# The tail h - tanh(h) of a feed-forward layer: a product of two shifted squares from ScalarE in place of a Horner chain on VectorE, and no GpSimd

## The chip, the cores and the metric

The kernel runs on one core of one Trainium2 chip. The metric is the device time of one execution in microseconds (us). Before the change three runs took 1145.72, 1147.4 and 1150.55 us; the median is 1147.4 us. One execution was recorded by the hardware profiler, and all rows below come from it. The engines are named as the profile does: PE is TensorE's matmul, PEld its weight load, DVE VectorE, ACT ScalarE, POOL GpSimd, SP the engine that issues the DMAs.

## The reference, cut to what matters

```
state = zeros(B, H, D, D)                           # B, H, S, D = 4, 8, 768, 48
for t in range(S):                                  # linear attention with a decay per feature
    y[t]  = r[t] @ (state + (u * k[t]) outer v[t])
    state = w[t][:, None] * state + k[t] outer v[t]
x = y, as (B*S, H*D) = (3072, 384)
h = x @ w_in                                        # w_in: 384 x 2048
g = h - tanh(h)
out = g @ w_out                                     # w_out: 2048 x 384
```

Everything is computed in float32. The difference h - tanh(h) loses its digits where h is small, so the kernel uses a series there.

## The kernel before, in words

There are four batches of 768 tokens. For each batch the attention runs over four pairs of heads. A pair computes its scores inside chunks of 128 tokens in levels m = 1, 2, 4, ... 64: at each level PE makes the score blocks (`gram`, L184), DVE takes them into the score matrix under a mask (`take`, L198; for m of 32 and 64 ACT does it with plain copies, L205), then DVE multiplies the decays into r (L219) and POOL into k (L221), and only after that the next level's `gram` can start. Then come transposes of k (L242), their copies by ACT (L243), the chunk states (L248 on PE, L255 and L257 on DVE) and the outputs `yp` (L266, L269), which ACT copies to `y_sb` (L272).

The feed-forward layer works on blocks of 384 tokens, two to a batch. `first` (L285) runs over 16 slices f of 128 hidden features: three float32 matmuls `hp` (L290; each is two passes in the trace, so six rows to a slice), the copy h by ACT (L293), and then the tail that the change touches (L295 to L309), which ends in a tile `gT`. `second` (L313) runs over three groups of 128 tokens: 16 matmuls `op` over all `gT` (L317), the copy `o` by ACT (L320), and the DMA out. PSUM for `hp` and `op` is one pool of two buffers (`ps_d`). The tiles of the tail (h, th, sq, big, o) have three buffers each, `gT` has 18.

The layer of batch b - 1 is laid between the attention of batch b: the first pair stands beside the first block's `first`, the second beside its `second`, and so on. So the execution has four stretches: batch 0's attention with the loading of the weights (about 0 to 206 us), then three batches of attention with the layer of the batch before (206 to 963 us), then the layer of the last batch alone (963 to 1144.7 us). Within a stretch the tile framework's scheduler decides at build time in which order each engine takes its instructions. Each engine then works through its list in that order and waits on semaphores, so an instruction that waits holds up all that stand behind it on its engine.

In this text an "hp stretch" is a stretch of the middle part in which `hp` is computed (beside an even pair), and an "op stretch" one in which `op` is computed (beside an odd pair). There are six of each.

## Time and profile before

| | us | what it is |
|---|---|---|
| median of three runs | 1147.4 | the metric |
| span of the profiled execution | 1144.7 | first to last instruction |
| PE busy | 953.4 (83%) | matmuls, pipelined |
| DVE busy | 849.5 (74%) | |
| POOL busy | 458.1 (40%) | 300.9 of it in L298, the subtraction h - tanh(h) |
| ACT busy | 302.6 (26%) | |
| DMA, mean of its engines | about 11% | q1 moved 40.90 MB |

A share of the whole span is a mean over stretches that differ. The stretch tables below give each engine's busy time in one stretch; the difference to the length of the stretch is that engine's idle time. In a row of instructions the bracket at its end says how long the engine was idle before it and what ended that.

### The profile page before, as it was taken

What the parts mean: (1) busy time and instruction counts of PE and PEld (TensorE: products, weight loads), DVE (VectorE), ACT (ScalarE), POOL (GpSimd) and SP (SyncE); (2) the same over time, 40 slices, a digit from 0 to 9 for tenths busy, and PEclk for the clock granted to TensorE, in tenths of its full rate; (3) what the DMA queues carried; (4) which work ended last, traced back from release to release, by engine and by line L of the source; (5) the groups of instructions that cost most, each with busy time, mean ns of one, the idle gap of its engine ahead of it and who ended that gap; (6) DMA issues with size and microseconds to landing.
All of it is one profiled execution on the core that took longest, in us unless ns stands there. A gap on an engine that the chain in (4) does not pass through costs nothing. (4 is left out here: it accounts for less than half of the span.)

```text
span 1144.7 us, 14496 instructions
## 1 busy us (share of the span) xinstructions
PE 953.4 (83%) x5464; PEld 648.1 (57%) x5464; DVE 849.5 (74%) x1688; ACT 302.6 (26%) x653; POOL 458.1 (40%) x292
## 2 busy tenths in 40 slices
PE   3867667898898879897999799888998789779778
PEld 3767667664565546664666457664666456335334
DVE  6776877899739992799659972899568962990991
ACT  1202112343023411343123401342123303330430
POOL 3332323347314531357223631357224811760670
PEclk9999999999899899998998879998999999899899
DMA  6222232200010002000010001000100000000000
GB/s 234 72 95 88 80 105 88 70 28 1 28 49 15 15 21 76 23 28 1 28 49 29 1 21 36 21 28 0 39 25 1 1 9 13 1 0 21 0 0 21
DMA packets 17749, 41.82 MB, mean 37 GB/s; under 512 B 1808, under 2 KB 7952, under 8 KB 17680
## 3 DMA queue, kind: packets, MB, share of 16 engines
q1 hardware_dynamic: 17680, 40.90, 10.8%
q8 instruction: 43, 0.70, 0.3%
q14 instruction: 26, 0.21, 0.1%
HBM read 36.18 MB, written 4.72 MB: 36 GB/s over the span
## 5 line engine op out<-in xcount | busy, mean ns | idle before, releaser
L298 POOL TENSOR_TENSOR th<-h,th 128x384 f32<-128x384 f32 x128 | 300.9, 2368 | 235.2 <-ACT th L295 235.1
L290 PE MATMUL hp<-xT,w_in_sb 128*128 128x384 f32 x768 | 306.7, 542 | 48.8 <-ACT h L293 48.8
L317 PE MATMUL op<-w_out_sb,gT 128*128 128x384 f32 x768 | 288.9, 525 | 32.9 <-DVE gT L309 16.5
L184 PE MATMUL g<-rp,kq 48*128 48x64 f32 x2304 | 185.0, 317 | 84.3 <-DVE rp L219 48.6
L184 PEld LDWEIGHTS g<-rp,kq 48*128 48x128 f32 x2304 | 171.7, 228 | 132.6 <-issue 69.3
L290 PEld LDWEIGHTS hp<-xT,w_in_sb 128*128 128x128 f32 x768 | 148.5, 206 | 154.8 <-ACT h L293 70.2
L304 DVE SCALAR_TENSOR_TENSOR gT<-gT,sq 128x384 f32<-128x384 f32 x384 | 230.3, 610 | 0.6
L317 PEld LDWEIGHTS op<-w_out_sb,gT 128*128 128x128 f32 x768 | 147.9, 202 | 138.9 <-DVE gT L309 27.3
L221 POOL TENSOR_TENSOR kq<-kq,tot 128x384 f32<-128x384 f32 x96 | 98.0, 1021 | 206.8 <-PE g L184 196.3
L293 ACT COPY h<-hp 128x384 f32<-128x384 f32 x128 | 61.3, 479 | 254.2 <-DVE gT L307 136.2
L198 DVE COPY_PREDICATED scores<-mask,g 128x384 f32<-128x384 uint8 x128 | 79.1, 677 | 66.5 <-PE g L184 64.7
L309 DVE COPY_PREDICATED gT<-big,th 128x384 f32<-128x384 int32 x128 | 97.2, 759 | 18.9 <-POOL th L298 18.6
L300 DVE TENSOR_SCALAR big<-sq 128x384 int32<-128x384 f32 x128 | 68.9, 539 | 39.8 <-ACT sq L297 39.8
L304 DVE SCALAR_TENSOR_TENSOR gT<-sq 128x384 f32<-128x384 f32 x128 | 86.3, 674 | 0.0
L320 ACT COPY o<-op 128x384 f32<-128x384 f32 x24 | 11.5, 479 | 267.9 <-PE op L317 267.9
L219 DVE TENSOR_TENSOR rp<-rp,tot 128x384 f32<-128x384 f32 x96 | 56.1, 584 | 30.9 <-PE g L184 30.7
L221 POOL TENSOR_TENSOR kq<-kq,wt 128x384 f32<-128x384 f32 x16 | 19.5, 1217 | 148.3 <-ACT h L293 62.4
L198 DVE COPY_PREDICATED scores<-mask_even,g 128x384 f32<-128x384 uint8 x32 | 31.0, 1024 | 54.5 <-PE g L184 54.1
L307 DVE SCALAR_TENSOR_TENSOR gT<-gT,h 128x384 f32<-128x384 f32 x128 | 71.0, 555 | 0.2
L295 ACT ACTIVATE th<-h 128x384 f32<-128x384 f32 x128 | 65.9, 515 | 16.3 <-DVE gT L309 15.4
L297 ACT ACTIVATE sq<-h 128x384 f32<-128x384 f32 x128 | 66.5, 519 | 2.6
L269 PE MATMUL yp<-v_sb,scores 128*128 128x48 f32 x384 | 64.6, 298 | 0.0
(54 smaller groups left out, 755.2 us busy)
## 6 DMA issues: line engine op xcount, KB each, us to landing
kq<-in_kT SPq DMA_DIRECT2D x16, 384.0 KB, 3.1
rp<-in_rT SPq DMA_DIRECT2D x16, 384.0 KB, 3.0
wt<-in_wT SPq DMA_DIRECT2D x16, 384.0 KB, 3.1
raw<-in_w_in SPq DMA_DIRECT2D x12, 512.0 KB, 3.9
raw<-in_w_out SPq DMA_DIRECT2D x16, 384.0 KB, 3.1
v_sb<-in_v SPq DMA_DIRECT2D x4, 1152.0 KB, 6.8
out_y<-o SPq DMA_DIRECT2D x24, 192.0 KB, 1.9
u_sb<-in_uT SPq DMA_DIRECT2D x1, 2.0 KB, 1.6
```

The lines of the kernel that those rows point to most:

```text
L184: nc.tensor.matmul(g[h][:, c, :].rearrange("s (b m) -> s b m", m=m), lhsT=lhs[rows, c * L:(c + 1) * L], rhs=rhs, start=True, stop=True)
L198: nc.vector.copy_predicated(out=dst, mask=mask, data=src)
L221: nc.gpsimd.tensor_tensor(out=kv, in0=kv, op=ALU.mult, in1=right.unsqueeze(2).to_broadcast([P, nblk, m]))
L290: nc.tensor.matmul(hp, lhsT=w_in_sb[:, kc, f * P:(f + 1) * P], rhs=xT[:, kc, :], start=(kc == 0), stop=(kc == KC - 1))
L295: nc.scalar.activation(out=th, in_=h, func=AF.Tanh)
L297: nc.scalar.activation(out=sq, in_=h, func=AF.Square)
L298: nc.gpsimd.tensor_tensor(out=th, in0=h, in1=th, op=ALU.subtract)
L300: nc.vector.tensor_single_scalar(big, sq, SMALL, op=ALU.is_gt)
L304: nc.vector.scalar_tensor_tensor(out=g, in0=prev, scalar=c / SERIES[-1], in1=sq, op0=ALU.add, op1=ALU.mult)
L307: nc.vector.scalar_tensor_tensor(out=g, in0=g, scalar=SERIES[-1], in1=h, op0=ALU.mult, op1=ALU.mult)
L309: nc.vector.copy_predicated(out=g, mask=big, data=th)
L317: nc.tensor.matmul(op, lhsT=gs[f][:, i * P:(i + 1) * P], rhs=w_out_sb[:, f, :], start=(f == 0), stop=(f == NF - 1))
```

## The change

Only the tail of `first`, and with it some buffers, is changed. For |h| under 0.5 the old code evaluates a polynomial of degree 4 in s = h * h by Horner's rule: four instructions of the form (x + c) * s and one that multiplies by c4 and h, all on DVE, after a comparison s > 0.25 on DVE which makes the mask; ACT computes tanh and the square; POOL computes h - tanh(h); and DVE puts that difference where the mask is set.

The new code factors the polynomial into two quadratics, each written as a square with a shift plus a constant. ACT computes qa = (s + a1)^2 and qb = (s + a2)^2 with a bias that is read from a small tile, and the mask as Relu(s - 0.25), whose bits are nonzero where s is over 0.25. DVE does three multiplications (c4 * h * s, then times qa + b1, then times qb + b2), the difference h - tanh(h), and the masked copy. POOL has nothing left in the layer. Line numbers grow by 4 to 6 in the new file.

```diff
 SMALL = 0.25
-SERIES = (0.33333332796974213, -0.13333225818814606, 0.05393347775205225,
-          -0.02147073784982366, 0.0069430510383758255)
+SERIES = 0.0069430510383758255
+QUAD = ((0.6848211999739032, 6.0837500747262405), (-2.2310245716004378, 2.349190352486121))
...
+    shift = const.tile([P, 3], F32, name="shift", tag="shift")
+    for i, value in enumerate((QUAD[0][0], QUAD[1][0], -SMALL)):
+        nc.vector.memset(shift[:, i:i + 1], value)
...
-            h = dense.tile([P, NB], F32, name="h", tag="h")
+            def new(name):
+                return dense.tile([P, NB], F32, name=name, tag=name)
+
+            h, th, s, qa, qb, big = (new(n) for n in ("h", "th", "s", "qa", "qb", "big"))
             nc.scalar.copy(out=h, in_=hp)
-            th = dense.tile([P, NB], F32, name="th", tag="th")
+            nc.scalar.activation(out=s, in_=h, func=AF.Square)
+            nc.scalar.activation(out=qa, in_=s, func=AF.Square, bias=shift[:, 0:1])
+            nc.scalar.activation(out=qb, in_=s, func=AF.Square, bias=shift[:, 1:2])
             nc.scalar.activation(out=th, in_=h, func=AF.Tanh)
-            sq = dense.tile([P, NB], F32, name="sq", tag="sq")
-            nc.scalar.activation(out=sq, in_=h, func=AF.Square)
-            nc.gpsimd.tensor_tensor(out=th, in0=h, in1=th, op=ALU.subtract)
-            big = dense.tile([P, NB], I32, name="big", tag="big")
-            nc.vector.tensor_single_scalar(big, sq, SMALL, op=ALU.is_gt)
+            nc.scalar.activation(out=big, in_=s, func=AF.Relu, bias=shift[:, 2:3])
+            hs = new("hs")
             g = gpool.tile([P, NB], F32, name="gT", tag="gT")
-            prev = sq
-            for c in SERIES[-2::-1]:
-                nc.vector.scalar_tensor_tensor(out=g, in0=prev, scalar=c / SERIES[-1], in1=sq,
-                                               op0=ALU.add, op1=ALU.mult)
-                prev = g
-            nc.vector.scalar_tensor_tensor(out=g, in0=g, scalar=SERIES[-1], in1=h,
+            nc.vector.scalar_tensor_tensor(out=hs, in0=h, scalar=SERIES, in1=s,
                                            op0=ALU.mult, op1=ALU.mult)
-            nc.vector.copy_predicated(out=g, mask=big, data=th)
+            nc.vector.scalar_tensor_tensor(out=hs, in0=qa, scalar=QUAD[0][1], in1=hs,
+                                           op0=ALU.add, op1=ALU.mult)
+            nc.vector.scalar_tensor_tensor(out=g, in0=qb, scalar=QUAD[1][1], in1=hs,
+                                           op0=ALU.add, op1=ALU.mult)
+            nc.vector.tensor_tensor(out=th, in0=h, in1=th, op=ALU.subtract)
+            nc.vector.copy_predicated(out=g, mask=big.bitcast(I32), data=th)
...
-            o = dense.tile([P, DM], F32, name="o", tag="o")
+            o = dense.tile([P, DM], F32, name="o", tag="hs")
```

The scheduler puts the new instructions into the lists as follows. First ACT's list near the end of the first block of the last batch's layer, before the change: three instructions to a slice.

```order
L293 COPY h<-hp 128x384
L297 ACTIVATE sq<-h 128x384
L295 ACTIVATE th<-h 128x384
L293 COPY h<-hp 128x384
L297 ACTIVATE sq<-h 128x384
L295 ACTIVATE th<-h 128x384
L320 COPY o<-op 128x384 x3
```

The same place after the change: the copies h of two slices stand together, and the five instructions of each slice follow behind both.

```order
L300 COPY h<-hp 128x384 x2
L301 ACTIVATE s<-h 128x384
L304 ACTIVATE th<-h 128x384
L302 ACTIVATE qa<-s,shift 128x384
L303 ACTIVATE qb<-s,shift 128x384
L305 ACTIVATE big<-s,shift 128x384
L301 ACTIVATE s<-h 128x384
L304 ACTIVATE th<-h 128x384
L302 ACTIVATE qa<-s,shift 128x384
L303 ACTIVATE qb<-s,shift 128x384
L305 ACTIVATE big<-s,shift 128x384
```

So the copies of slices 14 and 15 stand behind the full work of slices 0 to 13, and the work of the last two slices stands behind them. In all of the last batch's first block ACT has 96 instructions where it had 48.

Second PE's list where the first block's `hp` goes over into its `op`, with the attention's matmuls of the second pair of batch 1 between (uk, kmix and kq are the three forms of k that `gram` takes), before the change:

```order
L184 MATMUL g<-rp,uk 128x64 x9
L184 MATMUL g<-rp,kmix 128x64 x12
L290 MATMUL hp<-xT,w_in_sb 128x384 x15
L317 MATMUL op<-w_out_sb,gT 128x384 x23
L184 MATMUL g<-rp,kq 128x64 x12
L317 MATMUL op<-w_out_sb,gT 128x384 x3
```

The same place after the change:

```order
L188 MATMUL g<-rp,uk 128x64 x9
L188 MATMUL g<-rp,kmix 128x64 x4
L294 MATMUL hp<-xT,w_in_sb 128x384 x6
L188 MATMUL g<-rp,kmix 128x64 x8
L323 MATMUL op<-w_out_sb,gT 128x384 x11
L188 MATMUL g<-rp,kq 128x64 x12
L323 MATMUL op<-w_out_sb,gT 128x384 x3
```

The long run of `hp` at the end is cut, and the next pair's first level on kq stands behind 11 matmuls of `op` and no longer behind 23. In the last batch's layer PE's list is as it was: 48 `hp`, 48 `op`, 48 `hp`, 48 `op`, with a few transposes ahead.

## Rows read from the trace of the kernel before

**Rows 1.** Stretch table: PE, PEld, DVE, ACT, POOL busy us; clock; last row six hp stretches.
```profile
334.40:402.50 68.10, 57.83 (x386) 38.30 (x385) 63.85 (x119) 27.28 (x58) 32.77 (x20) 0.95 0.06 21
...
sum 420.10, PE 353.38 PEld 233.79 DVE 383.93 ACT 164.90 POOL 216.62; mean PE 58.90 PEld 38.97 DVE 63.99 ACT 27.48 POOL 36.10
```

**Rows 2.** The same table, two of the six op stretches and the sum of six.
```profile
656.00:718.00 62.00, 59.74 (x319) 39.30 (x319) 30.69 (x69) 9.92 (x24) 16.03 (x9) 0.86 0.09 29
788.00:841.00 53.00, 50.65 (x297) 33.02 (x297) 31.01 (x68) 7.17 (x18) 16.04 (x9) 0.95 0.09 31
...
sum 336.90, PE 315.50 PEld 205.31 DVE 187.16 ACT 47.89 POOL 92.12; mean PE 52.58 PEld 34.22 DVE 31.19 ACT 7.98 POOL 15.35
```

**Rows 3.** Waits over the span: who waited for whom, us in total, times, longest.
```profile
ACT h L293 <- DVE gT L307: 136.2, 65, 5.2
...
ACT y_sb L272 <- PE yp L269: 97.5, 32, 8.6
...
ACT scores L205 <- PE g L184: 55.6, 27, 6.1
...
PE hp L290 <- ACT h L293: 48.8, 30, 3.9
...
PE op L317 <- DVE gT L309: 16.5, 14, 1.8
```

**Rows 4.** Chain that ended last, last batch's layer: start, us, engine, tile, line.
```profile
967.97 0.49 ACT h L293
...
1029.80 25.23 PE op L317 x68
1055.03 3.47 PE hp L290 x11
...
1121.79 19.63 PE op L317 x60
1141.44 0.48 ACT o L320
```

**Rows 5.** Groups by line: busy us, mean ns of one, idle us before.
```profile
L298 POOL TENSOR_TENSOR th<-h,th 128x384 f32<-128x384 f32 x128 | 300.9, 2368 | 235.2 <-ACT th L295 235.1
...
L304 DVE SCALAR_TENSOR_TENSOR gT<-gT,sq 128x384 f32<-128x384 f32 x384 | 230.3, 610 | 0.6
...
L300 DVE TENSOR_SCALAR big<-sq 128x384 int32<-128x384 f32 x128 | 68.9, 539 | 39.8 <-ACT sq L297 39.8
...
L295 ACT ACTIVATE th<-h 128x384 f32<-128x384 f32 x128 | 65.9, 515 | 16.3 <-DVE gT L309 15.4
...
L293 ACT COPY h<-hp 128x384 f32<-128x384 f32 x128 | 61.3, 479 | 254.2 <-DVE gT L307 136.2 <-PE hp L290 74.7 <-POOL th L298 38.6
...
L219 DVE TENSOR_TENSOR rp<-rp,tot 128x384 f32<-128x384 f32 x96 | 56.1, 584 | 30.9 <-PE g L184 30.7
...
L173 ACT ACTIVATE kmix<-kq,u_sb 128x384 f32<-128x384 f32 x16 | 10.4, 650 | 9.3 <-PE g L184 9.3
```

**Rows 6.** Timeline of the last batch's first block: start us, duration us, instruction.
```profile
997.51 0.48 ACT L293 COPY h<-hp 128x384 f32<-128x384 f32 x1 [0.70 <-DVE gT L307]
998.03 0.52 ACT L297 ACTIVATE sq<-h 128x384 f32<-128x384 f32 x1
998.46 0.51 ACT L295 ACTIVATE th<-h 128x384 f32<-128x384 f32 x1
...
1000.88 0.55 DVE L307 SCALAR_TENSOR_TENSOR gT<-gT,h 128x384 f32<-128x384 f32 x1
1001.34 0.55 DVE L304 SCALAR_TENSOR_TENSOR gT<-gT,sq 128x384 f32<-128x384 f32 x1
...
1004.92 1.37 DVE L309 COPY_PREDICATED gT<-big,th 128x384 f32<-128x384 int32 x1 [0.89 <-POOL th L298]
1006.19 1.34 DVE L304 SCALAR_TENSOR_TENSOR gT<-gT,sq 128x384 f32<-128x384 f32 x1
```

**Rows 7.** Timeline, start of the hp stretch that begins at 334.40 us.
```profile
339.54 0.48 ACT L293 COPY h<-hp 128x384 f32<-128x384 f32 x1 [1.50 <-PE hp L290]
```

## The prediction

> **What bounds the kernel now.** I read the stretch tables first. In the middle part (206 to 963 us) PE is on average the busiest engine in the op stretches, and DVE in the hp stretches. An hp stretch takes 70.0 us on average (420.1 / 6) and PE is busy for 58.9 of them, so it stands for 11.1; DVE is busy for 64.0 [rows 1]. An op stretch takes 56.2 us (336.9 / 6), PE is busy for 52.6, DVE for 31.2 [rows 2]. So the hp stretches are the place where PE waits for something, and DVE is what is nearly full there.
>
> The waits say what it is. Over the span PE stood 48.8 us in front of `hp` for the copy h of ACT, and that copy stood 136.2 us for L307, the last arithmetic of the tail on DVE [rows 3]. That chain is a loop through buffers: `hp` needs a PSUM buffer, which the copy h frees; the copy needs one of three tiles h, which DVE frees when it is through with a slice. So PE goes at the pace of DVE's tail once its lead of about five slices is used up. A second sign is the 16.5 us that `op` stood for the last `gT` [rows 3].
>
> The chain of waits shows the same loop undisturbed, in the last batch's layer, where no attention stands beside it. The first copy h starts at 967.97, and the last `gT` of that block releases `op` at 1029.80: 61.8 us for 16 slices, 3.86 us to a slice [rows 4]. ACT's three instructions take about 1.5 us of these, so ACT is idle for more than half [rows 5, 6].
>
> **DVE and POOL.** The tail has seven DVE instructions to a slice, and on the timeline one follows the other after 0.46 us when nothing disturbs (1000.88 to 1001.34), but after 1.27 us where POOL's subtraction runs beside it (1004.92 to 1006.19) [rows 6]. Seven steps of 0.46, with a short one for the comparison, are about 3.1 us; the rest up to 3.86 is what the two engines cost each other. POOL's own subtraction shows a mean of 2368 ns [rows 5].
>
> After the change DVE has five: three of the same form, a TENSOR_TENSOR, and the masked copy. A TENSOR_TENSOR of this shape on DVE has a mean of 584 ns where the other form has 610 [rows 5], so I give it the same step. That is 5 x 0.46 = 2.3 us to a slice, with no POOL subtraction beside it: 1.5 us less than the pace of 3.86. The multiplications of k stay on POOL, so beside attention some of DVE's steps stay long.
>
> **ACT.** It gets six instructions to a slice in place of three. Without an operand from a tile the steps are 0.52 us (h to the square, which waits for it) and 0.43 (square to tanh) [rows 6]. Three of the six read a bias from a tile, which no row of this size shows exactly. From below such a step costs 0.43 like the tanh; from above the nearest row is L173, an ACTIVATE of 128x384 with a scale from a tile and with strides, 650 ns against 515 for the tanh, so 0.135 more [rows 5], and if the steps did not overlap at all, 0.65. I take 0.1 more than the tanh, since part of L173's surplus may be its strides: 0.53 a step. The slice then costs 0.52 + 2 x 0.43 + 3 x 0.53 = 2.97, and as the copies stand in pairs one wait is saved now and then: 2.95 us. The bounds are 2.67 (no surcharge) and 0.52 + 2 x 0.43 + 3 x 0.65 = 3.33; with every instruction at its full mean and no overlap, 0.48 + 2 x 0.52 + 3 x 0.65 = 3.47. So the loop's pace falls from 3.86 to 2.95 us, and its bound moves from DVE (then 2.3) to ACT.
>
> The Trainium skill, "ScalarE: Activation LUTs", section "Rules for kernel authors", says to put relu, add and multiply on VectorE, not on ScalarE; by that rule the mask and the two squares go the wrong way. The trace's row for the comparison on DVE, 539 ns, is no dearer than an ACT instruction, which bears the rule out for the mask [rows 5]. The same page, section "What ACT_TABLE_LOAD costs", gives an ACTIVATE with a pointer bias 280 ns + 0.833 ns per element and an overlap of 93 ns; as an estimate from that page the step is 0.507 us and the slice 2.9, so the sum would be about 1 us less per block. That rule speaks for a better split of the same work; it does not turn the sign, since it is ACT that had time to spare.
>
> **The last batch's layer.** Its first block: the copy of slice 14, after which `op` gets its PSUM buffer, comes after 14 slices of ACT work, 967.97 + 14 x 2.95 + 0.5 = 1009.8. `op` is 96 passes, in the trace's undisturbed row 60 of them take 19.63 us, 0.327 each [rows 4], so 31.4 us and an end at 1041.2, in place of 1055.03. The last `gT` is due at 967.97 + 16 x 2.95 + 1.2 = 1016.4, and `op` reaches it 15 x 0.65 = 9.8 us after its start, at 1019.6, so it does not wait. Gain 13.8. Second block: from the start of `hp` to the end of `op` the old time is 1141.44 - 1055.03 = 86.4 [rows 4]; the new one is 2.5 (six passes and a handoff) + 41.3 + 0.5 + 31.4 = 75.7. Gain 10.7. Together 24 us. `op` is PE alone and nothing of it is saved: that is why 0.9 us a slice over 32 slices, 29 us, does not all come out.
>
> **The middle.** In an hp stretch ACT has, up to the copy of slice 14, 14 x 2.95 = 41.3 us of the tail, and an attention pair's copies, which the op stretches bound at about 7.1 us, as one row of them shows 7.17 us of ACT work in all [rows 2]. The first copy comes 5.1 us after the start (339.54 against 334.40) [rows 7]. ACT takes its list in order, so it also stands where an attention copy waits for PE: now 97.5 us for the outputs and 55.6 for the scores over 16 pairs [rows 3], 9.6 to a pair; being busier it will arrive later, and I take 6. Sum 5.1 + 41.3 + 7.1 + 6 = 59.5, to which I add 1 for handoffs in a list that is now tight: 60.5 in place of 70.0. PE's own 58.9 is the floor just below, so little more is to be had. Six times 9.5 is 57.
>
> In the op stretches PE is bound, and stays so. ACT's last slices spill over into it, and the next pair's first level now stands behind 11 `op` and not 23, which lets the scores start earlier but puts DVE's decay of r behind the tail of slice 14; PE has 7 to 11 matmuls to bridge that, 5 to 7 us, about what the last slices need. The 16.5 us for the last `gT` shrink. I count 3 for all six.
>
> **What costs nothing.** The three memsets of `shift` stand at the start on DVE, long before the first copy h. The tile `o` now shares the ring of hs, so a slice's hs waits for an old output's DMA; the ring was last used a whole block before. Stretch 0 to 206 us has no instruction of the tail. Relu needs no further table: the built list of ACT has one table load, as before.
>
> **Sum.** 57 + 3 + 24 = 84 us. The profiled execution spans 1144.7, the median of the runs is 1147.4, 2.7 more, so 1147.4 - 84 = 1063 us.
>
> **The rivals.** *ACT's list holds the attention back.* ACT now is nearly full in the hp stretches, its copies for the scores, k and y stand behind tail instructions of slices that are not urgent, and PE waits for these copies in front of L248 and L266 rather than for h. For it: the order is fixed at build time with other durations than the chip's. Against: the waits now named L205 and L272 are ACT waiting for PE, not the reverse [rows 3]. If half of the gain in the hp stretches is lost so, and all in the op stretches: 28 + 24 = 52, 1095 us. Chance 0.24.
>
> *PE is never short and keeps its full clock.* Op stretches took 53 us at a mean granted clock of 0.95 and 62 at 0.86 [rows 2]; full is 2.4 GHz and the lower level 1.2 GHz. What sets the clock off these rows don't show; if it is PE's stands before and if they go, the op stretches all take 53: 336.9 - 318 = 19 us. With hp stretches at 57 (the 58.9 with some of it run at the low clock) 78 us, and 26 at the end: 123, 1024 us. Chance 0.13.
>
> *ACT becomes a worse bound than DVE was.* The place is the same loop. Per hp stretch the sum 5.1 + 14 x + 13.1 reaches 70.0 at x = 3.7 us a slice, and in the last batch `op` would start no sooner than the old 1055.03 - 31.4 at x = 3.96; about 3.75 decides, 0.62 us to an ACT instruction. The dearest sum from rows is 3.47, which gives 66.8 and so a gain of 3.2 x 6 + 10 = about 29, 1118 us. For a loss the bias would have to cost more than any row shows: at x = 4.2 each hp stretch takes 7 us more and each last block about 3.5, 42 + 7 = 49 us slower, 1196. Chance 0.05. *No effect*, because PE's stands return in other places: 1147, chance 0.03.
>
> **How the numbers follow.** My forecast has 0.55, the rivals 0.24, 0.13, 0.05 and 0.03. Predicted is 1063 us. The range 1030 to 1102 holds the forecast with both bounds of the bias at nearly their full width and the first rival, and leaves out most of the second and the two that are not faster, about 0.2. A difference under 0.5% (6 us) can't be told from none here. Faster 0.92, same 0.03, slower 0.05.
>
> **What would show it.** ACT's three instructions with a bias at about 0.6 us and steps of 0.53; in the last batch copies h of two slices every 5.9 us and the first `op` near 42 us after the first copy; DVE's steps of the tail at 0.46 throughout there; PE's wait for the copy h, where it is left, ended by ACT's own list and no longer by L307; hp stretches near 60 us and op stretches unchanged. It is wrong if an hp stretch keeps over 65 us, if a slice costs ACT over 3.4, or if PE's waits are named after L205, L243 or L272.

## The result, and the profile after

The changed kernel takes 1042.7 us (median of 4 runs, 1037.1 to 1048.1), the kernel before beside it 1146.6: a ratio of 0.911, 95% interval 0.902 to 0.920. Predicted were 1063 us. The runs of the changed kernel lie at two levels, about 1037 at a mean granted clock of 0.972 and about 1048 at 0.961; the profiled one is of the upper level (1048.07, span 1046.4).

The busy line of the page, kernel after (share of the span, number of instructions):

```profile
PE 924.0 (88%) x5464; PEld 648.8 (62%) x5464; DVE 676.7 (65%) x1435; ACT 479.7 (46%) x1037; POOL 174.5 (17%) x164
```

The span shrank by 98.3 us, of which 29.4 are PE's busy time (953.4 before) with the same 5464 instructions, and 69 are waits. The mean granted clock of the profiled execution was 0.948 before and is 0.961 now, so more of the same passes ran at the full clock.

The stretch table of the kernel after (PE, PEld, DVE, ACT, POOL busy, granted clock), sum of the six hp stretches:

```profile
sum 356.80, PE 334.70 PEld 229.33 DVE 301.24 ACT 276.51 POOL 61.46; mean PE 55.78 PEld 38.22 DVE 50.21 ACT 46.08 POOL 10.24
```

The same view, kernel after, its op stretches: the first of the six, the second, and the sum:

```profile
265.30:332.50 67.20, 64.34 (x340) 43.39 (x338) 24.66 (x57) 12.30 (x27) 7.07 (x7) 0.77 0.09 27
389.10:441.90 52.80, 50.33 (x291) 33.44 (x290) 22.38 (x51) 11.54 (x27) 8.00 (x7) 0.94 0.16 53
...
sum 333.90, PE 318.73 PEld 213.81 DVE 134.88 ACT 71.81 POOL 45.67; mean PE 53.12 PEld 35.63 DVE 22.48 ACT 11.97 POOL 7.61
```

The hp stretches went from 420.1 to 356.8 us [rows 1], the op stretches from 336.9 to 333.9 [rows 2], the last batch's layer (895.6 to 1046.4 us, before 962.8 to 1144.7) from 181.9 to 150.8. ACT's busy time in the hp stretches went up from 165 to 277 us and DVE's went down from 384 to 301. The first op stretch stands out: 67.2 us at a mean clock of 0.77. From 280 to 310 us the granted clock was 0.50, although PE was busy in all of these 30 us. Where a stretch ends can be set a few us earlier or later; with the end of the last `op` as the border in both kernels, the hp stretches lose 64.8 us and the op stretches 2.4.

Waits over the span, kernel after (who for whom: us in total, times, longest):

```profile
ACT h L300 <- PE hp L294: 45.3, 45, 2.2
...
PE g L188 <- DVE rp L223: 31.5, 22, 3.0
...
PE g L188 <- POOL kq L225: 18.9, 10, 2.3
...
PE hp L294 <- ACT h L300: 13.9, 12, 1.3
```

The loop that the prediction found is gone. The 136.2 us in which the copy h stood for DVE's tail [rows 3] have no row any more; the copy now waits for PE, and PE stands 13.9 us for the copy h in place of 48.8. What is left in front of PE is the attention's. Of the 31.5 us for rp, 25.1 lie before 205 us, where nothing was changed. PE's waits in the middle alone, kernel after (205 to 895.6 us), are led by kq from POOL:

```profile
PE g L188 <- POOL kq L225: 13.5, 6, 2.3
PE g L188 <- issue: 9.4, 6, 2.1
PE g L188 <- DVE rp L223: 6.4, 8, 1.9
```

The row "issue" is the stand at the start of the op stretches, shown below. No row there names the copy h: all 13.9 us for it lie in the last batch's layer. Beside attention PE never stands for ACT's tail.

The groups by line, kernel after (busy us, mean ns of one, idle us before it):

```profile
L302 ACT ACTIVATE qa<-s,shift 128x384 f32<-128x384 f32 x128 | 78.3, 612 | 0.0
...
L310 DVE SCALAR_TENSOR_TENSOR hs<-qa,hs 128x384 f32<-128x384 f32 x128 | 70.3, 550 | 2.2 <-ACT qa L302 2.2
...
L304 ACT ACTIVATE th<-h 128x384 f32<-128x384 f32 x128 | 66.3, 518 | 0.0
...
L300 ACT COPY h<-hp 128x384 f32<-128x384 f32 x128 | 57.4, 476 | 45.4 <-PE hp L294 45.3
```

An ACT instruction with a bias from a tile takes 612 ns against 518 without; DVE's form that took 610 ns [rows 5] takes 550 now that no POOL subtraction runs beside it.

Timeline of ACT in the last layer, kernel after (start, duration, instruction; rows of other engines are left out):

```profile
911.85 0.83 ACT L300 COPY h<-hp 128x384 f32<-128x384 f32 x2
...
912.57 0.53 ACT L301 ACTIVATE s<-h 128x384 f32<-128x384 f32 x1
...
913.00 0.52 ACT L304 ACTIVATE th<-h 128x384 f32<-128x384 f32 x1
...
913.41 0.61 ACT L302 ACTIVATE qa<-s,shift 128x384 f32<-128x384 f32 x1
...
913.92 0.61 ACT L303 ACTIVATE qb<-s,shift 128x384 f32<-128x384 f32 x1
...
914.42 0.61 ACT L305 ACTIVATE big<-s,shift 128x384 f32<-128x384 f32 x1
...
914.93 0.52 ACT L301 ACTIVATE s<-h 128x384 f32<-128x384 f32 x1
...
917.27 0.84 ACT L300 COPY h<-hp 128x384 f32<-128x384 f32 x2
```

ACT is never idle here. Two copies h take 0.72 us together (911.85 to 912.57), s to th is 0.43, th to qa 0.41, and each step behind an instruction with a bias 0.50 to 0.51. A pair of slices takes 917.27 - 911.85 = 5.42 us, 2.71 to a slice.

Timeline of PE in the last layer, kernel after:

```profile
917.79 4.14 PE L294 MATMUL hp<-xT,w_in_sb 128*128 128x384 f32 x12 [1.29 <-ACT h L300]
...
939.54 31.23 PE L323 MATMUL op<-w_out_sb,gT 128*128 128x384 f32 x96 [1.30 <-ACT h L300]
...
1011.57 31.23 PE L323 MATMUL op<-w_out_sb,gT 128*128 128x384 f32 x96 [1.30 <-ACT h L300]
```

PE takes two slices in 4.14 us and then stands 1.30 for ACT, ten times in all: 5.44, ACT's pace.

Then the start of an op stretch in the middle, kernel after, DVE and PE rows of the timeline:

```profile
730.58 4.68 PE L323 MATMUL op<-w_out_sb,gT 128*128 128x384 f32 x14
...
736.20 0.56 DVE L312 SCALAR_TENSOR_TENSOR gT<-qb,hs 128x384 f32<-128x384 f32 x1
...
736.67 0.56 DVE L223 TENSOR_TENSOR rp<-rp,wt 128x384 f32<-128x384 f32 x1
...
737.33 2.83 PE L188 MATMUL g<-rp,kq 48*128 48x64 f32 x24 [2.08 <-issue]
...
740.09 5.50 PE L323 MATMUL op<-w_out_sb,gT 128*128 128x384 f32 x10
745.52 1.55 PE L188 MATMUL g<-rp,kq 48*128 48x64 f32 x24
```

and the table of 2 us stretches there (length, PE, PEld, DVE, ACT, POOL, clock, DMA):

```profile
736.00:738.00 2.00, 0.67 (x7) 0.70 (x8) 2.00 (x6) 1.57 (x4) 0.00 (x0) 0.84 0.00 0
738.00:740.00 2.00, 2.00 (x21) 1.97 (x20) 1.37 (x3) 0.00 (x0) 1.71 (x1) 0.50 0.78 194
...
746.00:748.00 2.00, 2.00 (x23) 1.61 (x22) 0.90 (x2) 0.00 (x0) 0.74 (x1) 1.00 0.00 0
```

This is a place that the prediction treated too lightly. PE has run out of `op` matmuls and stands 2.08 us. The profile names no releaser, but the multiplication rp, which the attention's passes read, ends at 737.23, 0.1 us before PE goes on, and DVE was full before it (2.00 of 2.00): rp stands in DVE's list behind the tail of slices. When PE goes on, the granted clock is 0.50, the lower of its two levels (1.2 GHz, not 2.4): 24 passes of g take 2.83 us in place of 1.55, and ten `op` passes 5.50. From 737.33 to 745.52 are 8.2 us; at the full clock they would be 1.55 + 10 x 0.327 = 4.8. So after the stand of 2 us here the lower clock costs about 3.4 more. The other op stretches have such a stand too, of 1.7 to 1.9 us; after one of them (624.45 us) the clock stayed at 1.00.

A second place of this kind lies in every hp stretch, in the attention. POOL and PE rows of the timeline there, kernel after:

```profile
352.20 3.57 POOL L225 TENSOR_TENSOR kq<-kq,tot 128x384 f32<-128x384 f32 x1 [2.76 <-PE g L188]
...
355.83 1.55 PE L188 MATMUL g<-rp,kq 48*128 48x64 f32 x24 [2.32 <-POOL kq L225]
```

POOL's multiplication of kq takes 3.57 us here and 0.86 to 1.21 for its neighbours in the same stretch. While it stands, DVE goes through rp and the tail one step after the other, 0.46 to 0.48 us apart, from 352.19 to 355.08; POOL ends 0.7 us after DVE stops. PE stands 2.32 us for kq, and soon after the granted clock falls to the lower level (0.62 in 358 to 360 us). The six hp stretches have one such stand each, 1.85 to 2.33 us, 13.5 in all. The change took POOL out of the layer, but not out of the attention beside it.

### The profile page after: what moved, and what is told of

Same layout as the page of the kernel before. It is cut to its first block, busy times and chain, and to the rows that moved or that the text cites. A ratio compares the mean times of both kernels' runs of the same rounds, so it can differ in the third digit from the quotient of the medians.

```text
span 1046.4 us, 14715 instructions
## 1 busy us (share of the span) xinstructions
PE 924.0 (88%) x5464; PEld 648.8 (62%) x5464; DVE 676.7 (65%) x1435; ACT 479.7 (46%) x1037; POOL 174.5 (17%) x164
## 5 line engine op out<-in xcount | busy, mean ns | idle before, releaser
L294 PE MATMUL hp<-xT,w_in_sb 128*128 128x384 f32 x768 | 279.2, 507 | 13.9 <-ACT h L300 13.9
L188 PE MATMUL g<-rp,kq 48*128 48x64 f32 x2304 | 190.5, 324 | 85.1 <-DVE rp L223 31.5
L202 DVE COPY_PREDICATED scores<-mask,g 128x384 f32<-128x384 uint8 x128 | 80.2, 679 | 64.8 <-PE g L188 63.0
L308 DVE SCALAR_TENSOR_TENSOR hs<-h,s 128x384 f32<-128x384 f32 x128 | 75.0, 586 | 59.0 <-ACT s L301 58.9
L312 DVE SCALAR_TENSOR_TENSOR gT<-qb,hs 128x384 f32<-128x384 f32 x128 | 75.8, 592 | 7.0 <-ACT h L300 0.5
L315 DVE COPY_PREDICATED gT<-big,th 128x384 f32<-128x384 int32 x128 | 77.2, 603 | 4.7 <-ACT th L304 0.5
L209 ACT COPY scores<-g 32x192 f32<-32x192 f32 (+1 forms) x96 | 33.2, 362 | 100.0 <-PE g L188 99.4
L303 ACT ACTIVATE qb<-s,shift 128x384 f32<-128x384 f32 x128 | 78.3, 612 | 0.1
L302 ACT ACTIVATE qa<-s,shift 128x384 f32<-128x384 f32 x128 | 78.3, 612 | 0.0
L305 ACT ACTIVATE big<-s,shift 128x384 f32<-128x384 f32 x128 | 78.2, 611 | 0.0
L310 DVE SCALAR_TENSOR_TENSOR hs<-qa,hs 128x384 f32<-128x384 f32 x128 | 70.3, 550 | 2.2 <-ACT qa L302 2.2
L314 DVE TENSOR_TENSOR th<-h,th 128x384 f32<-128x384 f32 x128 | 70.5, 551 | 0.0
```

Of the source, the lines that this page charges most:

```text
L188: nc.tensor.matmul(g[h][:, c, :].rearrange("s (b m) -> s b m", m=m), lhsT=lhs[rows, c * L:(c + 1) * L], rhs=rhs, start=True, stop=True)
L202: nc.vector.copy_predicated(out=dst, mask=mask, data=src)
L294: nc.tensor.matmul(hp, lhsT=w_in_sb[:, kc, f * P:(f + 1) * P], rhs=xT[:, kc, :], start=(kc == 0), stop=(kc == KC - 1))
L302: nc.scalar.activation(out=qa, in_=s, func=AF.Square, bias=shift[:, 0:1])
L303: nc.scalar.activation(out=qb, in_=s, func=AF.Square, bias=shift[:, 1:2])
L305: nc.scalar.activation(out=big, in_=s, func=AF.Relu, bias=shift[:, 2:3])
```

## The experiments

**Theory A:** the change moved the loop's bound from DVE to ACT's list, so the time that is left in the hp halves is ACT's. **Rivals:** the gain is mostly that GpSimd's subtraction is gone, not the polynomial; and in the middle it is another list, or PE itself, that bounds.

For each run the table gives the median, its ratio to the kernel before on the same chip, and two stretches of its profiled execution: the middle five pairs of an hp and an op stretch (the first pair left out, because of that 0.77), with the part in which PE was busy, and the last batch's layer.

| run | us | ratio (95%) | five pairs (PE busy) | last layer |
|---|---|---|---|---|
| before | 1146.6 | 1 | 625.6 (553.4) | 181.9 |
| after | 1042.7 | 0.911 (0.902 to 0.920) | 563.1 (531.2) | 150.8 |
| e1 | 1075.9 | 0.936 (0.932 to 0.940) | 582.9 (524.6) | 164.4 |
| e8 | 1164.5 | 1.018 (1.014 to 1.022) | 634.6 (545.0) | 191.7 |
| e11 | 1169.3 | 1.020 (1.011 to 1.029) | 634.0 (539.9) | 190.4 |
| e2 | 1058.8 | 0.921 (0.915 to 0.927) | 572.5 (528.9) | 157.6 |
| e5 | 1046.7 | 0.914 (0.910 to 0.918) | 562.9 (530.0) | 164.8 |
| e4 | 985.9 | 0.857 (0.854 to 0.861) | 531.7 (515.9) | 136.9 |
| e9 | 1001.6 | 0.879 (0.875 to 0.884) | 530.3 (510.7) | 150.6 |
| e10 | 1008.0 | 0.885 (0.881 to 0.889) | 549.1 (523.1) | 137.3 |
| e3 | 1014.9 | 0.883 (0.878 to 0.887) | 558.8 (533.0) | 139.9 |
| e6 | 1013.3 | 0.886 (0.880 to 0.891) | 562.9 (531.0) | 130.5 |
| e7 | 1001.7 | 0.873 (0.865 to 0.881) | 555.2 (526.4) | 130.5 |

The order of the instructions is fixed at build time from assumed durations, so an edit to the slice also moves attention passes across the border of hp and op stretches. I therefore compare pairs of stretches, and a difference between two runs of the table is that of the edit with its new order. In the five pairs PE's passes lie in the same stretches as in the kernel after in all runs but two: in e5 48 and in e9 24 attention passes of each pair moved from the op to the hp stretch. How closely the five pairs repeat, e6 shows: it changes only the last layer, and its five pairs take 562.9 us against 563.1.

### What GpSimd's subtraction cost: e1, e2, e8, e11

e1 changes one line of the kernel before:

```diff
-            nc.gpsimd.tensor_tensor(out=th, in0=h, in1=th, op=ALU.subtract)
+            nc.vector.tensor_tensor(out=th, in0=h, in1=th, op=ALU.subtract)
```

> The kernel before with one edit: the subtraction h - tanh(h) goes from POOL to DVE. Theory A (POOL's subtraction slows DVE's steps from 0.46 to 1.27 us while it runs, about 0.8 us to a slice, and an eighth DVE step costs 0.46): pace 7 x 0.46 + 0.27 = 3.5 us to a slice in place of 3.86, the last batch's layer about 10 us shorter, each hp stretch about 4: 1112 us, between 1100 and 1130. Rival B (POOL's part is nearly the whole gain): 1040 to 1075. Rival C (POOL costs DVE nothing, so an eighth step only adds): 1160 to 1180.

It gave 71 to 75 us, although DVE has one instruction more for each slice: far more than theory A allowed, and at the edge of B. The pace of theory A did come out where it can be seen alone: the two hp halves of the last layer take 47.8 and 47.5 us against 52.3 and 51.9, about 0.3 us less to a slice. What it lacked is PE's clock: of the 68.2 us by which the span fell, 43.9 are PE's busy time for the same 5464 passes, at a mean granted clock of 0.989 against 0.948. DVE's rows, kernel e1, last layer:

```profile
930.87 0.55 DVE L298 TENSOR_TENSOR th<-h,th 128x384 f32<-128x384 f32 x1
931.34 0.55 DVE L304 SCALAR_TENSOR_TENSOR gT<-gT,sq 128x384 f32<-128x384 f32 x1
931.81 0.35 DVE L300 TENSOR_SCALAR big<-sq 128x384 int32<-128x384 f32 x1
932.08 0.55 DVE L304 SCALAR_TENSOR_TENSOR gT<-gT,sq 128x384 f32<-128x384 f32 x1
```

Each step is 0.46 or 0.47 us and the comparison 0.27: seven and one make 3.5 us to a slice against 3.86 before. No step of 1.2 us or more, as stood in [rows 6], is left there.

e2 puts the same subtraction of the changed kernel back on GpSimd:

```diff
-            nc.vector.tensor_tensor(out=th, in0=h, in1=th, op=ALU.subtract)
+            nc.gpsimd.tensor_tensor(out=th, in0=h, in1=th, op=ALU.subtract)
```

> The changed kernel with the subtraction back on POOL, all else as changed. Theory A (ACT's six instructions, 2.72 us to a slice, set the pace; DVE with four steps and POOL's interference needs about 2.6): last batch's layer as in the changed kernel, 149 us, hp stretches 0 to 3 us longer: 1045 to 1062 us. Rival B (it is the empty POOL that brought the gain): 1090 or more.

It cost 16 us, within theory A's range, though not quite where A had it: the last layer was to stay as it was and took 6.8 us more, the five pairs 9.4. So the two halves of the change overlap: the old polynomial with POOL out of the layer (e1) gives 6.4%, the new one with POOL still in it (e2) 7.9%, both together 8.9%. Two groups by line, kernel e2:

```profile
L314 POOL TENSOR_TENSOR th<-h,th 128x384 f32<-128x384 f32 x128 | 150.4, 1175 | 284.2 <-ACT th L304 257.3 <-DVE gT L315 12.9 <-PE g L188 8.7
...
L310 DVE SCALAR_TENSOR_TENSOR hs<-qa,hs 128x384 f32<-128x384 f32 x128 | 93.0, 726 | 12.5 <-ACT qa L302 5.9
```

L310 on DVE takes 726 ns here and 550 without. The same GpSimd subtraction takes 1175 ns beside this loose DVE and 2368 beside the full one [rows 5]: each holds the other up.

e8 and e11 are e1 with GpSimd doing work that nobody wants. In e8 it reads h itself; in e11 a copy in a ring of six:

```diff
             nc.vector.tensor_tensor(out=th, in0=h, in1=th, op=ALU.subtract)
+            pace = many.tile([P, NB], F32, name="pace", tag="pace")
+            nc.scalar.copy(out=pace, in_=h)
+            nc.gpsimd.tensor_tensor(out=junk, in0=pace, in1=w_out_sb[:, f, :], op=ALU.subtract)
```

> The kernel before with the subtraction on VectorE, and beside it a subtraction on GpSimd of the same size for each slice that reads h and a weight and writes a spare tile that nothing reads. It tells why taking the subtraction off GpSimd alone gave 6 per cent. Theory A (while GpSimd works, VectorE's steps are held up: the same instruction took about .46 us with GpSimd idle and up to 1.2 beside it): VectorE's chain of a slice is as long as before or longer by the subtraction, 1130 to 1165 us. Theory B (VectorE's chain waited for GpSimd's result, 2.4 us a slice, and that wait is gone): nothing waits for the spare tile, so 1076 to 1090 us.

> The kernel before with the subtraction on VectorE, and a GpSimd subtraction of the same size for each slice whose result nobody reads, as in the run with spare work; but it now reads a copy of h that ScalarE makes for it in a ring of six tiles, so that neither VectorE nor ScalarE's copy h waits for GpSimd unless it is six slices late. In the run before it held the three tiles h (ScalarE's copy h stood 87 us for it). Theory A (GpSimd's work beside VectorE's is enough: VectorE's steps, .46 us with GpSimd idle, come 1.2 to 1.4 us apart while it works): VectorE's tail stays near 4 us a slice, 1120 to 1155 us. Theory B (only a wait for GpSimd, for its result or for a tile that it still reads, costs time): 1076 to 1090 us. Between the two (both count): 1090 to 1120 us.

Both end slower than the kernel before, 89 and 93 us above e1, so GpSimd's work beside DVE costs that much with no wait for its result. e8 alone would not show that, because h is held until GpSimd has read it. The two runs do not show that such waits were worth nothing: in the kernel before DVE stood 18.6 us for th and the copy h 38.6 [rows 5], and e1 removed these too. A group by line of each of DVE and POOL, kernel e11:

```profile
L301 POOL TENSOR_TENSOR junk<-pace,w_out_sb 128x384 f32<-128x384 f32 x128 | 408.6, 3192 | 161.1 <-ACT pace L300 155.7
...
L307 DVE SCALAR_TENSOR_TENSOR gT<-gT,sq 128x384 f32<-128x384 f32 x384 | 232.1, 606 | 0.5
```

and the waits of e11:

```profile
ACT pace L300 <- POOL junk L301: 43.0, 8, 7.7
...
PEld g L184 <- POOL junk L301: 21.4, 16, 3.2
```

DVE is busy 900.3 us in e11, 829.5 in e1, with the same 1816 instructions: 71 us are steps that became longer. GpSimd's instruction takes 3192 ns on average; one stood 25 us (from 1083.47) while DVE went on at 0.47 a step. ACT's list still stood 43 us for the ring, and weight loads of the attention 21 behind GpSimd, so part of the 93 us is such waits; PE's busy time is 31.5 us above e1's as well, at a mean clock of 0.959. The shares I can't tell apart. e8 came out at the upper end of its theory A; e11's theory A (1120 to 1155) was too low, and theory B is out in both. The Trainium skill, "SBUF — State Buffer", section "Who interferes with whom", has a rule that fits: a VectorE instruction with two inputs in SBUF and a GpSimd instruction that reads SBUF share a port pair, and who is first holds it for the whole instruction. The traces agree on VectorE's side ([rows 6]: 1.37 and 1.34 us against 0.55); that one GpSimd instruction stands for 25 us, and in the kernel after for 3.57, beside a whole row of VectorE's goes beyond it.

### Which list bounds the hp halves: e5, e4, e9, e10

e5 issues the square qa twice:

```diff
             nc.scalar.activation(out=qa, in_=s, func=AF.Square, bias=shift[:, 0:1])
+            nc.scalar.activation(out=qa, in_=s, func=AF.Square, bias=shift[:, 0:1])
```

> The changed kernel with its qa activation issued twice, the same step with the same operands, so ScalarE carries one more step of about .505 us for each slice (96 x 2 slices). Theory A (ScalarE's list sets the stretches of hp slices, since the time between two slices there is ScalarE's 2.72 us): both the last layer and the six stretches beside the attention grow by 16 x .5 = 8 us for each half, so 2 x 8 + 6 x 8 = 64, about 1100 us (1085 to 1115). Theory B (only the last layer goes by ScalarE's list; the stretches beside attention go by TensorE, whose busy time there is 335 of 357 us, and ScalarE's 276 plus 6 x 8 = 325 still fits below it): 16 us in the last layer, 0 to 2 for each of the six stretches, 1058 to 1072 us.

(There are 128 slices, 16 to each of 8 halves; the 64 us are reckoned with these.) It came out at 1046.7 us. The last layer pays nearly in full, 150.8 to 164.8, and PE's stand there becomes 2.31 us for each pair of slices, as the timeline of PE in e5 shows:

```profile
978.73 4.14 PE L294 MATMUL hp<-xT,w_in_sb 128*128 128x384 f32 x12 [2.31 <-ACT h L300]
```

The five pairs pay nothing: 562.9 against 563.1 us. That is theory B, as far as the order allows: the hp stretches grew by 4 to 7 us with the passes that moved into them, and the op stretches shrank as much. The kernel after says the same without an edit, since PE has no wait for the copy h beside attention. So in the last layer ACT's list is the bound, beside attention it is not. The total lies 11 us below theory B's range because the part before the five pairs is 14.5 us shorter than in the profiled kernel after, whose first op stretch ran at 0.77.

e4 leaves out the Relu mask and the masked copy, so that large inputs keep the polynomial's value:

```diff
-            nc.scalar.activation(out=big, in_=s, func=AF.Relu, bias=shift[:, 2:3])
-            nc.vector.copy_predicated(out=g, mask=big.bitcast(I32), data=th)
```

> The changed kernel without the mask and without the masked copy, so that the series alone is the result at every h: ACT five instructions to a slice (2.21 us), DVE four (1.85 us). Theory A (hp stretches are at PE's floor, only the last layer is at ACT's pace): last layer 14 us shorter, hp stretches 1 to 2 us shorter each: about 1020 us. Rival (ACT's list sets the hp stretches too, 5 + 14 x + 13 with x down by 0.51): 7 us less in each, about 985 us.

985.9 us is the rival's number, and I took it for that at first: ACT's list was shorter, and the middle fell by 31 us in five pairs. But the edit takes a step from both lists, and e5 speaks against ACT. e9 and e10 take one each. e9 leaves out only the masked copy on DVE (the same values as e4); e10 only the Relu on ACT, its copy taking a fixed mask of zeros (again the polynomial's value everywhere):

```diff
# e9
-            nc.vector.copy_predicated(out=g, mask=big.bitcast(I32), data=th)
# e10
-            nc.scalar.activation(out=big, in_=s, func=AF.Relu, bias=shift[:, 2:3])
-            nc.vector.copy_predicated(out=g, mask=big.bitcast(I32), data=th)
+            nc.vector.copy_predicated(out=g, mask=keep, data=th)
```

> The changed kernel without the masked copy on VectorE, so large inputs keep the polynomial's value; ScalarE still makes the mask, which nothing reads. VectorE has one step of about .55 us less for each slice, ScalarE has the list of the changed kernel. It tells which list made leaving out both steps worth 57 us, where the last layer gave 14. Theory A (ScalarE's list lags at the end of each stretch of hp slices, and VectorE with it): 1030 to 1043 us, no stretch shorter by more than 1 us. Theory B (VectorE's list lags, and the attention's rp multiplication, which stands behind the slices' steps in it, comes late, so TensorE stands 2 us and then runs at half clock): the middle of the run falls by most of the 48 us, the last layer by nothing, 995 to 1012 us.

> The changed kernel without the Relu on ScalarE; the masked copy on VectorE stays and takes a mask of zeros made once, so large inputs keep the polynomial's value. ScalarE has one step of .505 us less for each slice, VectorE has the list of the changed kernel. Theory A (ScalarE's list lags): nearly all of the 57 us that leaving out both steps gave, 985 to 998 us. Theory B (VectorE's list lags): only the last layer gains, 32 slices x .45 = 14 us, 1020 to 1032 us.

The sums of the table over the five pairs, kernel after, then e4, e9 and e10:

```profile
sum 563.10, PE 531.17 PEld 360.39 DVE 358.02 ACT 287.32 POOL 87.28; mean PE 106.23 PEld 72.08 DVE 71.60 ACT 57.46 POOL 17.46
```

```profile
sum 531.70, PE 515.90 PEld 348.44 DVE 324.56 ACT 248.91 POOL 69.92; mean PE 103.18 PEld 69.69 DVE 64.91 ACT 49.78 POOL 13.98
```

```profile
sum 530.30, PE 510.73 PEld 347.05 DVE 328.38 ACT 286.95 POOL 74.00; mean PE 102.15 PEld 69.41 DVE 65.68 ACT 57.39 POOL 14.80
```

```profile
sum 549.10, PE 523.13 PEld 355.72 DVE 354.30 ACT 249.05 POOL 83.06; mean PE 104.63 PEld 71.14 DVE 70.86 ACT 49.81 POOL 16.61
```

DVE's step alone gives all that both gave in the middle (530.3 against 531.7) and nothing in the last layer (150.6). ACT's step alone gives all of the last layer (137.3 against 136.9) and 14 us in the middle, which theory B of e10 did not have: its 1020 to 1032 was missed by 12. The two do not add (33 and 14, together 31).

The two stands of the kernel after tell which part is whose. In e10 POOL's kq still takes 3.58 us in the five hp stretches, PE stands the same 11.6 us for it, and the hp stretches are not shorter; its gain lies in the op stretches (from the first to the last `op` 261.0 us in the kernel after, 244.3 in e10), where no stand before kq's `gram` is longer than 0.9 us. In e4 and e9, without the masked copy on DVE, the stand for kq is gone. POOL's row at the place of the 3.57 us, kernel e9:

```profile
335.44 1.14 POOL L225 TENSOR_TENSOR kq<-kq,tot 128x384 f32<-128x384 f32 x1 [2.76 <-PE g L188]
```

Theory B of e9 named only the stand for rp. In e9 PE still waits for rp after the first `op` matmuls, as its timeline shows, but for less:

```profile
693.07 4.14 PE L322 MATMUL op<-w_out_sb,gT 128*128 128x384 f32 x12
698.76 1.55 PE L188 MATMUL g<-rp,kq 48*128 48x64 f32 x24 [1.56 <-DVE rp L223]
```

After a stand of 1.56 us the 24 passes take 1.55, as they do at the full level. Of the 33 us that e9 gains in the five pairs, 20 are PE's busy time (531.2 to 510.7) and 12 its stands, as much as the 11.6 us for kq. So DVE's full list costs PE twice, through POOL's kq in the hp stretch and through rp at the start of the op stretch, and most of the price is paid in the clock. Part of e9's 33 may be the 24 passes that moved. From e10 to e4, where none moved, leaving out the masked copy gives 17.4 us, and the stand for kq goes.

The length of a stand alone does not say what the clock does. Another stand of e9, of 1.55 us (588.84), was followed by the lower level, and so were four of the six of e4 that took 1.08 or 1.09, as PE's timeline there shows:

```profile
483.67 1.56 PE L188 MATMUL g<-rp,kq 48*128 48x64 f32 x24 [1.08 <-issue]
485.16 3.89 PE L321 MATMUL op<-w_out_sb,gT 128*128 128x384 f32 x6
```

Six `op` passes take 3.89 us there, and 12 take 4.14 at the full level. In the last layer of e5 the granted clock was 1.00 from 963 to 1000 us, over stands of 2.31 us in every 6.45.

### Better splits: e3, e6, e7

e3 makes the mask on DVE:

```diff
-            nc.scalar.activation(out=big, in_=s, func=AF.Relu, bias=shift[:, 2:3])
+            nc.vector.tensor_single_scalar(big, s, SMALL, op=ALU.is_gt)
```

> The changed kernel with the mask made by a comparison on DVE in place of Relu on ACT. Theory A: ACT 2.21 us to a slice, DVE 5 x 0.46 + 0.27 = 2.6, so DVE sets the pace at 2.6: last batch's layer 3 us shorter, hp stretches unchanged within 2 us: 1035 to 1045 us. The rule of the Trainium skill, ScalarE: Activation LUTs, section Rules for kernel authors (relu and the like belong on VectorE), taken as it stands: ACT's 2.21 counts, 14 us less in the last layer, about 1028 us.

28 us better than the changed kernel, more than either theory allowed. 11 of them are in the last layer, between A's 3 and the rule's 14, so DVE's 2.6 us to a slice did not set the pace there; 4 are in the five pairs and 14 in the rest, where the kernel after had its stretch at 0.77. In place of 0.505 us on ACT it takes 0.27 on DVE (e1's rows). That is the rule of the Trainium skill, "ScalarE: Activation LUTs", section "Rules for kernel authors", which the prediction weighed: a relu belongs on VectorE; the runs agree, 1014.9 against 1042.7. One of e3's hp stretches took 72.1 us at a granted clock of 0.86, where its neighbour of the same kind took 60.0, so its five pairs are better than the table's 558.8 says. In that stretch one of POOL's kq multiplications took 4.05 us, and PE stood 3.4 for it; two hp stretches of e7 (65.8 and 65.7 us) show the same.

e6 interleaves `op` with `hp` in the last batch, three slices late, into three accumulators:

```diff
+            for f in range(NF + LAG):
+                if f < NF:
+                    gs.append(one_slice(xT, f))
+                if f >= LAG:
+                    for i in range(HC):
+                        nc.tensor.matmul(acc[i], lhsT=gs[f - LAG][:, i * P:(i + 1) * P],
+                                         rhs=w_out_sb[:, f - LAG, :],
+                                         start=(f == LAG), stop=(f == NF + LAG - 1))
```

> The changed kernel with the last batch's feed-forward layer in another order: three accumulators take each op slice three slices after its hp slice, so op passes fill TensorE's waits between hp slices, where the changed kernel runs 16 hp slices and then 96 op passes. Theory A (the last layer, 150 us of which TensorE is busy 130, goes by ScalarE's list in its hp halves, 43.9 and 41.0 us): TensorE's list becomes the bound there, about 125 to 132 us with the start, so 18 to 25 us less, 1017 to 1027 us. Theory B (ScalarE's list of 16 x 2.72 = 43.5 us a half is not what sets these halves, but the path through VectorE's chain of a slice): the op passes wait for gT of three slices before, and the layer stays within 8 us of 150, 1035 to 1046 us.

> The mask by a comparison on VectorE together with the fused last layer. Both act on the same waits of the last layer: the mask on VectorE left 140 us there with TensorE busy 131. Theory A (TensorE is the only bound of the last layer once op passes lie between the slices): 140 becomes 128 to 132, so 8 to 12 us below the 1015 of the mask alone, 1003 to 1008 us. Theory B (the two gains add, 28 + 20): about 995 us. A rival: VectorE's list, now 7 steps a slice, sets the fused layer: 16 x 2 x 3.5 = 112 plus the start of 13, no gain, 1013 to 1018 us.

PE's timeline in e6:

```profile
936.23 2.10 PE L294 MATMUL hp<-xT,w_in_sb 128*128 128x384 f32 x6
938.16 2.10 PE L329 MATMUL acc<-w_out_sb,gT 128*128 128x384 f32 x6
```

No wait is left, and the last layer takes 130.5 us, 20 less than after, as theory A said. The total fell by more, 29 us, and so lies 4 us below theory A's range, because e6's first op stretch ran at a clock of 0.94, in 56.8 us and not 67.2. That stretch has the same instructions in both kernels, so this is not the edit's. e7 has both edits. Its last layer is PE's 130.5 too, 9.4 under e3's, and it is the fastest kernel here that computes the whole reference: 1001.7 us (runs of 994.3, 997.1, 1006.2 and 1014.6), ratio 0.873, 0.865 to 0.881. Theory A's 1003 to 1008 holds within that scatter; that VectorE's list would leave no gain (1013 to 1018) is out.

## Why the prediction was right, point by point

The direction and the place held: DVE's tail paced the loop and its pace fell. The mechanism held in the last layer, where ACT became the bound of the hp halves. In the hp stretches of the middle, the largest term with 57 of 84 us, it did not: there the size came out by luck. Measured are 104 us, predicted were 84. The terms:

- **The pace before, 3.86:** the reading behind it is off, the number nearly right. At 1029.80 `op` has 68 of its 96 passes left [rows 4], so it was the fifteenth `gT` that released it and not the last; the sixteenth was done at 1032.65. From the end of the first `gT` (975.73) to that are 15 steps of 3.79 us.
- **DVE's five steps at 0.46:** held (L310 550 ns with a step of 0.46, against 610). What GpSimd's subtraction beside it cost was booked as the 0.75 us to a slice between 3.1 and 3.86. For the last layer's pace that was right, as e1's hp halves show. As the price of the whole it was too little: taking the subtraction alone off GpSimd gave 6.4%, with a step more on DVE, and 43.9 of the 68.2 us of span were PE's busy time, which the sum had only in the last layer's `op` (0.327 a pass).
- **ACT's slice, 2.95 us:** mis-sized, 2.71 measured. The surcharge for a bias was right (0.10 taken; 0.505 - 0.41 measured), and the Trainium skill's figure for it, 0.507 a step as an estimate from "ScalarE: Activation LUTs", section "What ACT_TABLE_LOAD costs", agrees with the trace to 0.01. The error lies in the copies h: I gave each 0.52 because its square waits for it [rows 6]; two that follow each other take 0.72 together, so 0.16 to a slice were too much. The rest is the three bias steps, 0.505 where I took 0.53, and the step after tanh, 0.41 and not 0.43.
- **The last layer, -24:** measured -31. From the first copy h (900.70) to the end of `op` at 970.77 are 70.1 us, predicted 73.2; the second block takes from 970.77 to 1042.80, 72.0, predicted 75.7 (86.4 before [rows 4]). Fourteen slices at 0.24 too much are 3.4 in each, which is all of it. `op` took 31.23, predicted 31.4.
- **The hp stretches, -57:** measured -63.3 (59.5 each, predicted 60.5). The size came out by luck, since the reason was not the one in the sum: 14 x 2.95 of ACT was to be the bound. PE never waits for the copy h there, and e5 shows that 0.5 us more for each slice on ACT costs nothing in a pair of stretches. PE was busy for 55.8 of the 59.5 us, and the stand for POOL's kq is 2.3 of the 3.7 that remain. The prediction had POOL's multiplications only as something that lengthens DVE's steps; that DVE's steps hold them up and PE waits for kq is no term of it.
- **The op stretches, -3:** -3.0 in the profiled run, where the first one at a clock of 0.77 hides about 10 more (e6), so the agreement is luck too. The prediction had DVE's decay rp behind the tail at the start of an op stretch and gave PE "7 to 11 matmuls to bridge that, 5 to 7 us, about what the last slices need". That step failed narrowly: PE had 14 passes, 4.7 us, stood 2.08, and then ran at the lower level for some 7 us.
- **The rivals:** ACT holding the attention back (1095) did not come; PE's remaining waits are for rp and kq, not for L209 or L276. The full clock (1024) came in part: PE's busy time fell by 29 us with its stands, and e9 and e4 show what the rest of that is worth. In the rival of ACT as a worse bound the 3.96 us should be 3.94, which changes nothing.

Open: how the 93 us of e11 divide between longer DVE steps, what is queued behind GpSimd and the clock; what, beside a stand, decides whether the clock falls; and why one op stretch ran at 0.77 and the same one in e6 at 0.94.

## What to carry to other kernels

Before moving arithmetic, look for an engine pair that slow each other: a step that reads 0.46 us alone and 1.3 beside a neighbour was worth more here than an instruction saved (e1 has one more on DVE and gains 6.4%). The pair slows both ways: what is left on GpSimd stands behind a full VectorE, and the wait turns up elsewhere, here in front of TensorE. When a bound is moved, work out the list of every engine at the border between two stages, not only its mean in a stage: 0.5 us more on ACT for each slice was free in the five pairs, and 0.5 less on DVE was worth 17 to 33 us there. Copies that stand in pairs cost less than two single ones with their waits.

## What the runs showed of the hardware that was not expected

- GpSimd and DVE: a 128x384 subtraction on GpSimd took a mean of 1175 ns beside a DVE with gaps, 2368 beside a full one and 3192 in e11, with single ones of up to 26.8 us; DVE's steps beside it went from 0.46 to 1.2 or 1.4 us in places. A multiplication of kq that takes about 1.1 us took 3.57 beside a row of DVE steps without a gap.
- The clock: after a stand of 2.08 us PE came back at the lower level and took 24 passes in 2.83 us and not 1.55; after one of 1.56 in e9 it came back at the full level, but one of 1.55 there and several of 1.08 in e4 were followed by the lower one. The stands of 1.30 us in every 5.44 of the last layer left the clock at 1.00. In the kernel after PE was at the lower level from 280 to 310 us, busy all the time.
- A comparison into an int32 mask on DVE has a step of 0.27 us, against 0.46 for the forms that read two tensors.
